# A squared-ReLU feed-forward block: x tile 0 loaded in two pieces, three tiles transposed ahead of chunk 0, shared tail transposes, a copy on ScalarE

## The chip, the cores and the metric

The kernel runs on one core of a Trainium2 chip. The metric is the device time of one execution in microseconds (us), smaller is better. Each kernel was executed several times; one execution of each was also recorded instruction by instruction (the profile, or trace). Loads are DMA transfers that an engine's queue issues: `nc.sync` is SyncE's queue (SPq in the traces), `nc.scalar` ScalarE's (ACTq). One execution below fell in a slow state, at a lower granted clock (0.853). Times in a trace count from the first instruction (the span); the device time is 1.8 to 2.0 us longer than the span.

## The reference

```python
B, S, D, F = 1, 2048, 576, 4608          # bf16: x, w1, b1, w2, b2
h = einsum("bsd,df->bsf", x, w1) + b1
r = where(h > 0, h, 0)
out = einsum("bsf,fd->bsd", r * r, w2) + b2
```

## The kernel before

Rows of x are worked on in four blocks of 512. The first product needs x transposed (D on the partitions). 576 is 4.5 times 128, so the last 64 rows of w1 ("tails") are handled by matmuls that use half of the array's rows, two at a time (64*128 in the timelines, where the others are 128*128; in the trace of before the first such pair, L203 and L205, starts at 9.849 and 9.853 us).

For the first block nothing is in SBUF (the on-chip memory that these loads fill) yet. An x tile is 128 rows of x. While the loads arrive, PE (the matrix engine) runs dummy matmuls (the warm-up), then transposes the four x tiles itself, and works off a first group of four 128-column output chunks, `k_outer`: for each 128 rows of D one `w1n` piece, in two halves of 256 x rows. Then come the rows of `a_rows(0)`: 16 steps `j`, each with 18 matmuls that take one 64-row half of the array each. Matmuls on the lower half (L188, later L196) read the piece of `w1_h` of half 0, those on the upper half (L190, later L198) the piece of half 1. Each step needs 288 KB of w1 and takes 1.94 us (nine pairs, 0.216 us apart in the trace of before).

```python
WARM = [512] * 6 + [128]                  # dummy matmuls on constants
...
load_x(nc.sync, 0)                        # 128 x 576 bf16, 144 KB
load_x(nc.scalar, 1)
load_w1n(nc.sync, 0)                      # 128 x 512 bf16, 128 KB
load_x(nc.scalar, 2)
load_w1n(nc.sync, 1)
load_x(nc.sync, 3)
for k in range(2, NK):
    load_w1n(nc.sync, k)
...
for (j0, j1) in [(0, 1), (1, 2), (2, 4), (4, 6), (6, 8), (8, 10), (10, 12)]:
    load_w1(nc.sync, 0, j0, j1)           # one half of the partitions each
    load_w1(nc.sync, 1, j0, j1)
    if j0 == 0:
        load_w1n8(nc.sync, 0)             # the tails of the first four chunks, 32 KB each
        load_w1n8(nc.sync, 1)
load_xT(1)                                # DMA transposes of the next x block
for (j0, j1) in [(12, 14), (14, 16)]:
    load_w1(nc.sync, 0, j0, j1)
    load_w1(nc.sync, 1, j0, j1)
...
# k_outer, in PE's order
for j in range(2):
    for k in range(NK): x_transpose(j, k)          # x tiles 0 and 1
for j in range(2):      x_transpose(j, NK)         # their tails
x_copies(0)
part(0, 0)                                         # four matmuls of 256 columns
for k in range(NK + 1): x_transpose(2, k)
part(0, 1); part(0, 2)
for k in range(NK + 1): x_transpose(3, k)
x_copies(1); dup_windows(0)                        # shifted copies, VectorE
part(0, 3); part(1, 0); make_b1T()
part(1, 1); part(1, 2); part(1, 3)
# then four tail matmuls, then a_rows(0)
```

## Time and profile before

| | before |
|---|---|
| device time | 290.71 us median of 3 (290.42 to 290.91) |
| the profiled execution | 291.46 us, span 289.6 |
| first transpose of PE | 3.77 us |
| first w1_h matmul | 10.29 us |

The first part of the page of the kernel before (engine, busy us and share, instructions) and the first line of its chain of waits:

```profile
PE 285.5 (99%) x2027; PEld 139.9 (48%) x2032; DVE 78.6 (27%) x176; ACT 96.7 (33%) x154; POOL 2.3 (1%) x10
...
PE 98%; DMA 1%; issue 0%; DVE 0%
```

PE is the whole kernel. The timeline of PE of the kernel before, in the head (start us, length us, engine, line, operation, output and inputs, shape, count; in brackets idle time of the engine before and what ended it):

```profile
0.78 2.83 PE L63 MATMUL wps<-const-bfloat16-1.0 128*128 128x512 bf16 x7 [0.78 <-PEq L344]
3.77 1.25 PE L149 MATMUL tb<-ident,x_sb 128*128 128x128 bf16 x10 [0.17 <-DMA x_sb<-in_x_dram]
4.87 1.01 PE L227 MATMUL pn<-xTw,w1n 128*128 128x256 bf16 x4
5.68 0.74 PE L149 MATMUL tb<-ident,x_sb 128*128 128x128 bf16 x5
6.21 1.19 PE L227 MATMUL pn<-xTw,w1n 128*128 128x256 bf16 x8
7.24 0.44 PE L149 MATMUL tb<-ident,x_sb 128*128 128x128 bf16 x5
7.51 1.04 PE L227 MATMUL pn<-xTw,w1n 128*128 128x256 bf16 x8
8.39 0.22 PE L166 MATMUL b1T_ps<-ident,b_rows 128*128 128x128 bf16 x1
8.44 1.47 PE L227 MATMUL pn<-xTw,w1n 128*128 128x256 bf16 x12
...
10.29 0.38 PE L188 MATMUL ph<-xTw,w_h 64*128 64x512 bf16 x1
```

Two things are to be read here. PE never waits long: after its first transpose no line has a wait in brackets. And the pace changes: five transposes take 0.74 us at 5.68 and 0.44 us at 7.24, four matmuls of 256 columns 1.01 us at 4.87, eight 1.04 us at 7.51. Single starts in the trace are 0.107 us apart for a transpose and 0.213 us for a 256-column matmul at first, and 0.056 and 0.109 later, about half of that: the document calls the first half clock and the second full clock. The trace's clock record begins at 6.51 us, with 1.00 ("the rise"); before that it holds nothing, so half clock is read from the steps. From 10.29 us to the last matmul (286.66 us) it takes 276.37 us.

Issues of loads on SyncE's queue (SPq) in the same trace; the `w_h` lines are the pieces of w1_h:

```profile
3.60 1.40 SPq L82 DMA_DIRECT2D w_h<-in_w_dram  x2
5.05 1.29 SPq L79 DMA_DIRECT2D w1n<-in_w_dram  x2
...
24.21 1.97 SPq L82 DMA_DIRECT2D w_h<-in_w_dram  x3
```

And, from the view of DMA issues of the kernel before in a window about 1.2 us, w1n piece 0 (size, us from issue to landing):

```profile
w1n<-in_w_dram SPq DMA_DIRECT2D x1, 128.0 KB, 3.1
```

It is issued at 1.20 and so lands at 4.3 us, before PE asks for it at 4.87. The queue's first w1_h piece is issued at 3.60 us, its last ones from 24.21 on.

### The profile page before, as it was taken

The page shows a single profiled execution, that of the slowest core. Times are in us where ns is not written, and L with a number is a line of the kernel's source. Part 1 is how long each engine was busy: PE and PEld are TensorE (multiplying, and loading weights), DVE is VectorE, ACT ScalarE, POOL GpSimd, SP SyncE. Part 2 cuts the span into 40 slices and gives each one's busy share as a digit, 9 for nine tenths or more (in the row PEclk, how much of TensorE's full clock was granted, in tenths as well). Part 3 has the DMA queues.
Part 4 walks back from the last instruction along what each step waited for, and adds up shares of the span by engine and source line. Part 5 has one row for each costly group of instructions (what it writes and reads, how often), then busy time and mean ns, then how long its engine had stood idle before and what let it go on. Part 6 is the DMA issues. An engine that isn't in the chain of part 4 may idle for free.

```text
span 289.6 us, 4693 instructions
## 1 busy us (share of the span) xinstructions
PE 285.5 (99%) x2027; PEld 139.9 (48%) x2032; DVE 78.6 (27%) x176; ACT 96.7 (33%) x154; POOL 2.3 (1%) x10
## 2 busy tenths in 40 slices
PE   8999999999999999999999999999999999999996
PEld 5544444444444555555544444444444455555555
DVE  1644554444500200000015444444440001100001
ACT  2566666666500000000027666666670000000000
POOL 3000000000000000000000000000000000000000
PEclk9999999999999999999999999999999999999999
DMA  7999999400001200000000000000000110000000
GB/s 198 221 245 188 308 389 212 92 0 2 0 14 25 52 16 18 16 16 18 16 16 2 1 2 0 2 0 2 0 2 0 36 38 16 16 16 19 33 16 18
DMA packets 31605, 16.52 MB, mean 57 GB/s; under 512 B 15700, under 2 KB 31584, under 8 KB 31584
## 3 DMA queue, kind: packets, MB, share of 16 engines
q1 hardware_dynamic: 31232, 15.91, 22.3%
q10 hardware_dynamic: 288, 0.30, 0.4%
q8 instruction: 16, 0.26, 0.4%
q14 instruction: 5, 0.04, 0.0%
q0 software_dynamic: 64, 0.01, 0.0%
HBM read 11.36 MB, written 2.36 MB: 47 GB/s over the span
## 4 chain that ended last, share of the span: by engine, by line
PE 98%; DMA 1%; issue 0%; DVE 0%
PE ph L188 42%; PE po L289 38%; PE pt L270 11%; PE pn L209 4%; PE pn L227 1%; DMA x_sb<-in_x_dram 1%; PE tb L149 1%; PE ph L190 1%; PE pn L203 1%; DVE o_sb L291 0%; PE b1T_ps L166 0%; PE pn L205 0%
## 5 line engine op out<-in xcount | busy, mean ns | idle before, releaser
L190 PE MATMUL ph<-xTw,w_h 64*128 64x512 bf16 x576 | 124.6, 376 | 0.0
L188 PE MATMUL ph<-xTw,w_h 64*128 64x512 bf16 x576 | 124.6, 376 | 0.0
L289 PE MATMUL po<-w_sb,hT 128*128 128x448 bf16 (+2 forms) x612 | 109.4, 341 | 0.0
L176 ACT ACTIVATE r<-ph,b1T 128x512 bf16<-128x512 f32 x128 | 81.1, 685 | 41.6 <-PE ph L190 41.6
L188 PEld LDWEIGHTS <-w_h 64*128 64x128 bf16 x576 | 54.1, 94 | 68.3
L289 PEld LDWEIGHTS <-hT 128*128 128x128 bf16 x612 | 58.5, 98 | 51.0
L177 DVE TENSOR_TENSOR hT<-r 128x512 bf16<-128x512 bf16 x144 | 61.2, 426 | 75.9 <-ACT r L176 75.5
L190 PEld LDWEIGHTS <-w_h 64*128 64x128 bf16 x576 | 54.1, 94 | 0.0
L291 DVE TENSOR_TENSOR o_sb<-po,b_bc 128x448 bf16<-128x448 f32 (+2 forms) x17 | 10.2, 597 | 125.8 <-PE po L289 125.8
L270 PE MATMUL pt<-hT,w_sb 128*128 128x512 bf16 x142 | 31.3, 379 | 0.1
L176 ACT ACTIVATE r<-pn,b1T 128x512 bf16<-128x512 f32 x16 | 10.3, 688 | 61.0 <-PE pn L205 59.6
L270 PEld LDWEIGHTS <-w_sb 128*128 128x128 bf16 x144 | 14.1, 98 | 17.0
L273 ACT ACTIVATE oT<-pt,b2T 128x512 bf16<-128x512 f32 x4 | 2.8, 688 | 28.3 <-PE pt L270 28.3
L209 PE MATMUL pn<-xTw,w1n 128*128 128x512 bf16 x45 | 10.4, 379 | 0.4 <-issue 0.3
L209 PEld LDWEIGHTS <-w1n 128*128 128x128 bf16 x48 | 4.5, 98 | 6.0 <-issue 0.8
L227 PE MATMUL pn<-xTw,w1n 128*128 128x256 bf16 x32 | 4.6, 295 | 0.0
L63 PE MATMUL wps<-const-bfloat16-1.0 128*128 128x512 bf16 (+1 forms) x7 | 2.8, 582 | 0.8 <-PEq L344 0.8
L227 PEld LDWEIGHTS <-w1n 128*128 128x128 bf16 x32 | 3.3, 107 | 0.5
L156 DVE COPY xTw<-tb 128x256 bf16<-128x256 bf16 x4 | 1.1, 292 | 6.7 <-PE tb L149 6.7
L119 DVE COPY xTw<-xTw 64x2048 bf16<-64x2048 bf16 x4 | 2.8, 690 | 0.2
L120 DVE COPY xTw<-xTw 64x2048 bf16<-64x2048 bf16 x4 | 2.7, 687 | 0.1
L149 PE MATMUL tb<-ident,x_sb 128*128 128x128 bf16 x20 | 2.4, 288 | 0.2 <-DMA x_sb<-in_x_dram 0.2
(23 smaller groups left out, 15.2 us busy)
## 6 DMA issues: line engine op xcount, KB each, us to landing
w_sb<-in_w_dram SPq DMA_DIRECT2D x4, 1296.0 KB, 12.7
w_h<-in_w_dram SPq DMA_DIRECT2D x14, 288.0 KB, 6.2
out_dram<-o_sb SPq DMA_DIRECT2D x15, 112.0 KB, 1.7
w_h<-in_w_dram SPq DMA_DIRECT2D x4, 144.0 KB, 3.5
w1n<-in_w_dram SPq DMA_DIRECT2D x4, 128.0 KB, 3.9
out_dram<-ot SPq DMA_DIRECT2D x4, 128.0 KB, 2.0
x_sb<-in_x_dram ACTq DMA_DIRECT2D x2, 144.0 KB, 2.9
x_sb<-in_x_dram SPq DMA_DIRECT2D x2, 144.0 KB, 3.4
```

The lines of the kernel that those rows point to most:

```text
L63: keep(nc.tensor.matmul(wps[:, 0:n], lhsT=ones[:, 0:P], rhs=ones[:, 0:n], start=True, stop=True))
L149: keep(nc.tensor.transpose(bank[:, slot, qc], xs[:, j, c0:c0 + P], ident[:]))
L176: keep(nc.scalar.activation(out=r[:], in_=bank[:], func=ACT.Relu, bias=b1T[:, ft:ft + 1], scale=1.0))
L177: keep(nc.vector.tensor_tensor(out=hTs[sb][:, ft, :], in0=r[:], in1=r[:], op=ALU.mult))
L188: keep(nc.tensor.matmul(bx[:], lhsT=w1_h[0:H, LO_C[i], jc], rhs=xT[0:H, LO_W[i], :], start=(i == 0), stop=(i == NC - 1)))
L190: keep(nc.tensor.matmul(by[:], lhsT=w1_h[H:P, UP_C[i], jc], rhs=xT[H:P, UP_W[i], :], start=(i == 0), stop=(i == NC - 1)))
L203: keep(nc.tensor.matmul(banks[2 * i][:], lhsT=w1n8[0:H, i, :], rhs=xT[0:H, SPC, :], start=start, stop=stop, skip_group_check=order == "k_o ...
L209: keep(nc.tensor.matmul(banks[g][:], lhsT=w1n[:, k, g * P:(g + 1) * P], rhs=xT[:, O + k, :], start=start, stop=stop))
L227: keep(nc.tensor.matmul(banks[g][:, hc], lhsT=w1n[:, k, g * P:(g + 1) * P], rhs=xT[:, O + k, hc], start=(h == 0 and k == 0), stop=False, s ...
L270: keep(nc.tensor.matmul(pt[:], lhsT=w2_sb[:, ft, DM:D], rhs=hT[:, ft, :], start=(i == 0), stop=(i == NFT - 1)))
L289: keep(nc.tensor.matmul(po[:, 0:d1 - d0], lhsT=hT[:, ft, jj * P:(jj + 1) * P], rhs=w2_sb[:, ft, d0:d1], start=(i == 0), stop=(i == NFT - 1)))
L291: keep(nc.vector.tensor_tensor(out=o_sb[:, d0:d1], in0=po[:, 0:d1 - d0], in1=b2_bc[:, d0:d1], op=ALU.add))
```

## The change

The intent is to start PE earlier and to take work and waits out of the head. x tile 0 comes in two column pieces on two queues; the warm-up is shorter to match; three x tiles are transposed before the first chunk, so that copies have time; the tail columns of two tiles share one transpose; a shifted copy moves to ScalarE. Loads are rearranged with it: more go through ScalarE's queue, `w1n8` is loaded in full for both halves (64 KB each) and ahead of `w1_h`, the last `w1_h` pieces and the w2 pieces are merged into larger ones, and b1 and b2 leave GpSimd's queue.

```diff
-    WARM = [512] * 6 + [128]
+    WARM = [512] * 5 + [256]
...
-    load_x(nc.sync, 0)
-    load_x(nc.scalar, 1)
-    load_w1n(nc.sync, 0)
+    load_x(nc.sync, 0, 0, 2 * P)
+    load_x(nc.scalar, 0, 2 * P, D)
+    load_x(nc.sync, 1)
     load_x(nc.scalar, 2)
-    load_w1n(nc.sync, 1)
-    load_x(nc.sync, 3)
-    for k in range(2, NK):
-        load_w1n(nc.sync, k)
+    load_w1n(nc.sync, 0, 1)
+    load_x(nc.scalar, 3)
+    load_w1n(nc.sync, 1, 2)
+    load_w1n(nc.scalar, 2, 3)
+    load_w1n(nc.sync, 3, 4)
...
+    keep(nc.scalar.dma_start(out=b1_rows[0:NFT, :], in_=b1.rearrange("(ft p) -> ft p", p=P)))
+    for h in range(2):
+        load_w1n8(nc.sync, h)               # now 64 KB each
...
+    def dup_windows_first():
+        keep(nc.scalar.copy(out=xT0[0:H, E:E + 3, :], in_=xT0[H:P, O:O + 3, :]))
+    def transpose_tails():
+        ... two transposes in place of four, four small copies, two shifted copies on VectorE
...
-                for j in range(2):
-                    for k in range(NK):
-                        x_transpose(j, k)
-                ...
+                for j in range(3):
+                    x_transpose(j)
                 part(0, 0)
-                for k in range(NK + 1):
-                    x_transpose(2, k)
+                x_transpose(3)
+                dup_windows_first()
                 part(0, 1)
                 part(0, 2)
-                ...
+                transpose_tails()
                 part(0, 3)
-                part(1, 0)
-                make_b1T()
-                for k in range(1, NK):
+                for k in range(NK):
                     part(1, k)
+                    if k == 1:
+                        make_b1T()
...
-        if j0 == 0:
-            load_w1n8(nc.sync, 0)
-            load_w1n8(nc.sync, 1)
     load_xT(1)
-    for (j0, j1) in [(12, 14), (14, 16)]:
+    for (j0, j1) in [(12, 16)]:
```

(Not shown here: the banks of PSUM, the layout of `w1n8`, the loads of b2 and w2.)

## The prediction

> **What bounds the kernel now.** The page's first part has PE busy 285.5 of 289.6 us (99%); the chain of work that ended last is 98% PE. From 10.29 us on (first L188 matmul in the timeline) 512-column matmuls start every 0.216 us until the last output. The change touches nothing there; w2 comes in three pieces instead of four, but is first used after 76 us. So only the head, 0 to 10.29 us, can change, plus new waits in the first rows.

> **The head before** (timeline, PE): warm-up matmuls 0.78 to 3.61; first transpose at 3.77, right after x tile 0 landed at 3.73 (3.0 us from issue). Then PE works nearly back to back until 10.29; its largest later gap is about 0.1 us, ahead of the L203 pair. Until about 6.5 us the steps are those of half clock (0.107 us per transpose, 0.213 per 256-column matmul), after it 0.056 and 0.109. [...] So the head is work-bound: 20+1 transposes, 32 half-width matmuls, 4 narrow ones.

> **What changes, costed.**
> - x tile 0 in two pieces on two queues: 144 KB instead of 288 KB ahead of the first transpose. From 2.9 to 3.7 us DMA moved about 350 GB/s, so an estimated 0.35 to 0.4 us less: first transpose at about 3.4. The shorter warm-up (ends about 3.1) fits. But this time is won at half clock: if the clock rises at 6.5 as before, 0.35 us earlier is worth about 0.18.
> - Two transposes fewer (19 against 21): 0.11 us.
> - Three tiles transposed ahead of chunk 0: no PE work removed, only waits, of which there is about 0.1 us. Tile 3 should land at about 5.0 instead of 6.1; it is wanted at about 5.6 to 6.1.
> - The shifted copy on ScalarE (64x1536) should take 1.4 to 1.9 us (estimate from its 0.376 us at 256 columns and 0.685 at 512) and end near 8.6 to 9.0; first read near 10.8. Off the chain. DVE's four tail copies (about 0.28 us each) end near 8.6, ahead of the pairs at about 9.5.
> - w1n8 is 128 KB instead of 64, ahead of w1_h, whose first pieces land up to 0.8 us later than 7.3 to 8, still before 9.9.
> - b1 is issued by ScalarE after its table load (about 4.0) and should land by 7 to 8; wanted at about 8.5.

> Sum on the critical path: 0.2 + 0.1 + 0.1, about 0.4 us; first w1_h matmul at about 9.9 instead of 10.29.

> **Prediction:** 290.3 us, 289.6 to 291.0 (8 in 10). Faster by over 2%: 0.005; within 2%: 0.985; slower by over 2%: 0.01. 2% would be 5.8 us, more than half of the head.

> **What would show it.** First transpose at 3.3 to 3.5 us; x tile 3 landed before 5.5; full-rate steps from about 6.5; no PE wait over 0.15 us after 4.5; first w1_h matmul at 9.7 to 10.1; from there to the end the same 279.3 us, to 0.2.

> **What would make it wrong.** The gap after the shorter warm-up, or waits for x tile 1, [...]. [...] the three timings before spread by 0.5 us, as much as the gain. PE waiting on b1 or w1n pieces. An early rise would make the gain larger, up to 0.8 us.

## The result, and the profile after

| | before | after |
|---|---|---|
| device time, median | 290.6 us (6 runs, 290.42 to 290.91) | 291.66 us (6 runs, 291.26 to 293.21) |
| ratio of the fast runs | | 1.0042, 95% interval 1.0020 to 1.0065 |
| the profiled execution | 291.46 us | 291.26 us |
| first transpose | 3.77 us | 3.07 us |
| first w1_h matmul | 10.29 us | 9.76 us |

Ratios here and below are the mean time of one kernel's fast runs over that of the other's fast runs of the same rounds, so they are not quite the ratio of the medians. The kernel became slower by 0.4%, clear of noise, and its times spread four times as far. The predicted 290.3 and the range to 291.0 were missed.

The page of the changed kernel, the same parts:

```profile
PE 285.5 (99%) x2029; PEld 139.4 (48%) x2029; DVE 79.3 (27%) x181; ACT 97.5 (34%) x153; POOL 1.5 (1%) x9
...
PE 97%; DMA 1%; SPq 0%; DVE 0%; issue 0%
```

The timeline of PE of the changed kernel in the head:

```profile
0.77 2.50 PE L63 MATMUL wps<-const-bfloat16-1.0 128*128 128x512 bf16 x6 [0.77 <-PEq L343]
3.07 1.64 PE L150 MATMUL tb<-ident,x_sb 128*128 128x128 bf16 x12
5.14 0.79 PE L232 MATMUL pn<-xTw,w1n 128*128 128x256 bf16 x4 [0.43 <-DMA w1n<-in_w_dram]
5.77 0.39 PE L150 MATMUL tb<-ident,x_sb 128*128 128x128 bf16 x4
5.99 1.04 PE L232 MATMUL pn<-xTw,w1n 128*128 128x256 bf16 x8
6.87 0.28 PE L163 MATMUL tl<-ident,xs 128*128 128x128 bf16 x2
6.98 1.47 PE L232 MATMUL pn<-xTw,w1n 128*128 128x256 bf16 x12
...
9.76 0.38 PE L196 MATMUL ph<-xTw,w_h 64*128 64x512 bf16 x1
```

PE starts 0.70 us earlier, but now it waits: 0.43 us without any work for w1n piece 0, and a little ahead of tile 1's transposes. In this execution the clock happened to rise at 5.55 us. The piece is issued at 1.66 us and lands at 5.1; from the view of DMA issues of the changed kernel about 1.65 us:

```profile
w1n<-in_w_dram SPq DMA_DIRECT2D x1, 128.0 KB, 3.4
```

The issues of SyncE's queue and what that queue waited for (waiter, what for: us in total, times, longest):

```profile
3.32 1.20 SPq L79 DMA_DIRECT2D w1n<-in_w_dram  x2
5.32 2.70 SPq L82 DMA_DIRECT2D w_h<-in_w_dram  x4
```

```profile
SPq L82 <- DMA x_sb<-in_x_dram: 0.8, 1, 0.8
```

The first piece of w1_h is issued at 5.32 us instead of 3.60 (and the merged last ones from 25.07, in the trace). Two w1n8 loads now stand ahead of it, and then the queue itself waits 0.8 us for an x tile to land. (In the same view of the kernel before, no load waits for a landing in this stretch.) The operands in the two traces show what this wait is. In the changed kernel that w1_h load waits for semaphore 106, which it then uses for its own completion; x tile 3's load, issued on ScalarE's queue at 1.66 us, has the same semaphore and landed at 5.30, and the w1_h load was issued at 5.32. (In after_look the same wait took 1.1 us.) In the kernel before the first w1_h load waits for semaphore 100, that of x tile 1, which had landed at 3.52 when the load was issued at 3.60. So between these two programs the landing that the first w1_h load has to wait for changed too. What comes of the later start is seen at step j = 12. PE's timeline of the kernel before there, where the two halves start together:

```profile
33.60 0.38 PE L188 MATMUL ph<-xTw,w_h 64*128 64x512 bf16 x1
33.60 0.38 PE L190 MATMUL ph<-xTw,w_h 64*128 64x512 bf16 x1
33.82 0.38 PE L188 MATMUL ph<-xTw,w_h 64*128 64x512 bf16 x1
```

and of the changed kernel:

```profile
33.06 0.38 PE L196 MATMUL ph<-xTw,w_h 64*128 64x512 bf16 x1
33.41 0.39 PE L198 MATMUL ph<-xTw,w_h 64*128 64x512 bf16 x1
33.41 0.39 PE L196 MATMUL ph<-xTw,w_h 64*128 64x512 bf16 x1
```

L198 should start with the L196 of 33.06. It starts 0.35 us later, when the merged piece of half 1 has landed (33.37 us in the trace). The lower half has run one step ahead by then and the two halves stay staggered until the next full-height matmul at 72.8 us, where the step is given back. From the first w1_h matmul to the last matmul it is 276.72 us instead of 276.37: the full 0.35 us.

So the fastest of the six executions shows 0.53 us won in the head and 0.35 us lost later. It doesn't show why the others took 291.5 to 293.2, nor why before's timed executions were faster than its profiled one. That was for the experiments.

### The profile page after: what moved, and what is told of

Read it like the earlier page. It is cut to its first block, busy times and chain, and to the rows that moved or that the text cites. A ratio compares the mean times of both kernels' runs of the same rounds, so it can differ in the third digit from the quotient of the medians.

```text
span 289.3 us, 4699 instructions
## 1 busy us (share of the span) xinstructions
PE 285.5 (99%) x2029; PEld 139.4 (48%) x2029; DVE 79.3 (27%) x181; ACT 97.5 (34%) x153; POOL 1.5 (1%) x9
## 4 chain that ended last, share of the span: by engine, by line
PE 97%; DMA 1%; SPq 0%; DVE 0%; issue 0%
PE po L287 38%; PE ph L196 29%; PE ph L198 14%; PE pt L268 11%; PE pn L217 4%; PE pn L232 1%; DMA w1n<-in_w_dram 1%; PE pn L211 1%; SPq L72 0%; PE pn L213 0%; DVE o_sb L289 0%; PE tb L150 0%; PE tl L163 0%; PE b1T_ps L174 0%
## 5 line engine op out<-in xcount | busy, mean ns | idle before, releaser
L198 PE MATMUL ph<-xTw,w_h 64*128 64x512 bf16 x576 | 124.8, 376 | 0.0
L196 PE MATMUL ph<-xTw,w_h 64*128 64x512 bf16 x576 | 124.8, 376 | 0.0
L196 PEld LDWEIGHTS <-w_h 64*128 64x128 bf16 x576 | 54.1, 94 | 46.9
L198 PEld LDWEIGHTS <-w_h 64*128 64x128 bf16 x576 | 54.0, 94 | 21.6 <-DMA w_h<-in_w_dram 0.5
L289 DVE TENSOR_TENSOR o_sb<-po,b_bc 128x448 bf16<-128x448 f32 (+2 forms) x17 | 10.2, 597 | 125.8 <-PE po L287 125.8
L213 PE MATMUL pn<-xTw,w1n 64*128 64x512 bf16 x8 | 2.4, 378 | 0.0
L211 PE MATMUL pn<-xTw,w1n 64*128 64x512 bf16 x8 | 2.4, 378 | 0.0
```

The costliest lines, as they stand in the source:

```text
L196: keep(nc.tensor.matmul(bx[:], lhsT=w1_h[0:H, LO_C[i], jc], rhs=xT[0:H, LO_W[i], :], start=(i == 0), stop=(i == NC - 1)))
L198: keep(nc.tensor.matmul(by[:], lhsT=w1_h[H:P, UP_C[i], jc], rhs=xT[H:P, UP_W[i], :], start=(i == 0), stop=(i == NC - 1)))
L211: keep(nc.tensor.matmul(banks[2 * i][:], lhsT=w1n8[0:H, 2 * i * P:(2 * i + 1) * P], rhs=xT[0:H, SPC, :], start=start, stop=stop, skip_grou ...
L289: keep(nc.vector.tensor_tensor(out=o_sb[:, d0:d1], in0=po[:, 0:d1 - d0], in1=b2_bc[:, d0:d1], op=ALU.add))
```

## The experiments

Four things are quoted from each trace: when the clock rose, the start of the first w1_h matmul, the time from it to the last matmul (276.37 us where nothing stalls), and the time of that execution. Medians are of 5 or 6 executions, each beside executions of the kernel before on the same chip (median 290.8 to 290.9 there).

| run | median us | ratio to before | profiled execution us | rise us | first w1_h us | to last matmul us |
|---|---|---|---|---|---|---|
| before | 290.6 | | 291.46 | 6.51 | 10.29 | 276.37 |
| after | 291.66 | 1.0042 | 291.26 | 5.55 | 9.76 | 276.72 |
| before_again | 290.89 | 1.0000 | (slow) | | | |
| after_again | 291.72 | 1.0024 | 292.98 | 8.87 | 11.81 | 276.37 |
| after_look | one run | | 293.25 | 9.15 | 11.77 | 276.67 |
| split_w1 | 293.37 | 1.0078 | 293.05 | 9.36 | 11.72 | 276.37 |
| before_merged | 291.38 | 1.0013 | 290.91 | 5.14 | 9.55 | 276.53 |
| fill_gaps | 292.32 | 1.0044 | 292.82 | 4.26 | 9.67 | 278.36 |
| before_newloads | 291.15 | 1.0010 | 290.99 | 3.92 | 9.67 | 276.37 |
| oldloads | 291.61 | 1.0023 | 291.80 | 5.96 | 9.89 | 277.12 |
| old_warmup | 292.05 | 1.0043 | 292.00 | no record; about 5.8 by the steps | 9.90 | 277.25 |
| w1_first | 291.52 | 1.0044 | 293.92 | see below | 12.59 | 276.37 |
| mended | 290.89 | 1.0006 | 291.33 | 6.77 | 10.20 | 276.37 |
| mended_fill | 291.96 | 1.0035 | 290.90 | 4.44 | 9.56 | 276.37 |
| mended_fill_look | one run | | 291.55 | 5.84 | 10.22 | 276.37 |
| before_w1late | 291.85 | 1.0028 | 292.04 | 6.79 | 10.41 | 276.80 |
| before_shortwarm | 291.97 | 1.0031 | 292.17 | 8.31 | 11.10 | 276.37 |
| early_w1n0 | 291.66 | 1.0023 | 291.66 | 4.31 | 10.46 | 276.37 |

### before_again and after_again: controls

No edit.

> Control: the kernel before, unchanged, timed against itself. Theory A (a real loss in the changed kernel: the merged last w1 pieces land too late) and theory B (the half-clock stretch of the changed kernel lasts longer in most executions): ratio 1.000, interval inside 0.999 to 1.001, median 290.4 to 290.8. Theory C (the changed kernel's times carry an offset of the measurement, because its six were taken another way than those of before): ratio about 1.003, median about 291.4.

> The changed kernel, unchanged, for its spread and a second trace. A: the trace again shows a gap of PE at the w1_h matmuls of j = 12 (about 33 us), of 0.1 to 2 us, differing from execution to execution; median 291.3 to 292, spread over 0.5 us. B: no or the same small gap at 33 us, but the half-clock stretch ends at another time than 5.5 us and the time goes with it. C: as before_again to 0.2 us.

before_again: ratio 1.0000 (0.9986 to 1.0014). One of its executions, the profiled one, slow (335.78 us, granted clock 0.853), is left out. The median, 290.89, lies a little above the expected 290.4 to 290.8, but so do the executions of before beside it (290.92). Theory C falls. after_again: the loss repeats (291.72, 1.0024, interval 1.0010 to 1.0039). Its trace, an execution of 292.98 us, has no gap at 33 us, but a rise at 8.87 us: B's picture. A's gap was not there. The changed kernel has at least two kinds of execution.

### split_w1: the last w1_h pieces in two again

```diff
-    for (j0, j1) in [(12, 16)]:
+    for (j0, j1) in [(12, 14), (14, 16)]:
```

> The changed kernel with the last w1 piece of each half loaded in two again (j 12 to 14, then 14 to 16), nothing else. A: no PE gap near 33 us, the pieces for j = 12 land before about 31.5, median 290.0 to 290.6, 0.8 to 1.5 us below after_again, spread below 0.4 us. B or C: the same as after_again to 0.2 us (in the profile at most the 0.35 us that the gap cost there comes back).

293.37 us, all five executions between 292.67 and 293.52: slower, not faster, and in the range of no theory. The traced one rose at 9.36 us and had no gap; as its first w1_h matmul came only at 11.72 us, that says little for the edit. A alone falls. Why all five came in the late kind, and only about three of twelve of the changed kernel, stays open; the edit touches nothing before 24 us.

### before_merged: the merged piece alone, in the kernel before

```diff
-    for (j0, j1) in [(12, 14), (14, 16)]:
+    for (j0, j1) in [(12, 16)]:
```

> The kernel before with the last w1 pieces merged as in the changed kernel, nothing else. The merged upper piece is issued at about 24.9 and should land at 31.5 to 33 us, wanted at 33.6. A: a stall in some executions only, median 290.6 to 291.4, spread larger than before_again's. B or C: the same as before_again to 0.2 us.

291.38 us, ratio 1.0013 (1.0000 to 1.0026): in A's range, near the edge of what can be told. Its trace was an early one (rise 5.14, first w1_h matmul 9.55), and there the stretch to the last matmul is 0.16 us longer than 276.37: a short stall at j = 12. This trace tells something else too: the same head as before, with the rise 1.37 us and the first transpose 0.25 us earlier, ends 0.74 us earlier, and the execution took 290.91 us. So before's profiled execution, with its rise at 6.51, was a late one of its kind.

### fill_gaps: PE kept busy where it waited

```diff
-                for j in range(3):
-                    x_transpose(j)
+                x_transpose(0)
+                fill(5)          # matmuls of 128 columns on constants, overwritten later
+                x_transpose(1)
+                x_transpose(2)
+                fill(8)
                 part(0, 0)
```

> The changed kernel with filler matmuls on constants (128 columns, results overwritten) in the two places where PE waited: five after the transposes of tile 0, eight ahead of chunk 0. No load is moved. B, now put so: the half-clock stretch ends at the end of the first 3.41 us window in which PE idles less than about 0.5 us (0.43 rose, 0.63 and 0.72 did not); the waits for x tile 1 and for w1n piece 0 cost the changed kernel that window in most executions. B expects the rise before 7 us in the trace, first w1_h matmul at 9.0 to 10.2, median 290.3 to 291.1 (0.7 to 1.5 below after_again), although PE has 13 matmuls more to do. If the waits cost only their own length, the fillers sit in their shadow and the median stays at 291.5 to 292.0.

The 3.41 us of B is the length of two stretches in the clock record of w1_first (below). Its idle times were read from traces: 0.43 us in after (PE busy 2.98 of the 3.41 us before its rise, 2.14 to 5.55), 0.63 in split_w1, 0.72 in after_again.

The rise came at 4.26 us and the first w1_h matmul at 9.67, as B wanted, and still the median was 292.32. The timeline of PE of fill_gaps says where the time went, at step j = 2:

```profile
13.55 0.38 PE L196 MATMUL ph<-xTw,w_h 64*128 64x512 bf16 x1
15.54 0.39 PE L198 MATMUL ph<-xTw,w_h 64*128 64x512 bf16 x1 [1.61 <-DMA w_h<-in_w_dram]
```

PE, early in the rows, ran into the w1_h supply and waited (the next step comes 1.99 us after the last); the piece landed at 15.49. So mending the clock alone brings the other loss out.

### before_newloads, oldloads, old_warmup: which part of the change

before_newloads puts the changed loads of x and w1n (order, queues, pieces) into the kernel before. oldloads puts those of before, and its warm-up, into the changed kernel. old_warmup puts only the warm-up length of before (`[512] * 6 + [128]`) into the changed kernel.

> The kernel before with only the changed order, queues and pieces of the x and w1n loads. B: PE idles 0.4 to 1.2 us ahead of chunk 0, waiting for w1n piece 0 (landing 5.1 to 6.0 instead of 4.0 to 4.3), the rise comes after 8 us in part of the executions, median 291.3 to 292.5, spread over 0.8. If the loss came from the changed order of PE's or the other engines' work: 290.5 to 291.0, as before.

> The changed kernel with the order and queues of the x and w1n loads, and the warm-up length, of before; everything else of the change stays. B: no PE wait over 0.3 us ahead of chunk 0, rise before 7 us, first w1_h matmul at 9.0 to 10.0, median 290.2 to 290.9. If the loss lies in the rest of the change: 291.4 or more.

> The changed kernel with the longer warm-up of before (6x512+128 columns instead of 5x512+256), nothing else. B: the wait for x tile 1 is filled (PE busy to about 4.0), the one for w1n piece 0 stays at 0.1 to 0.9 us, so fewer executions lose the window: median 290.6 to 291.5, below after_again's. If the shorter warm-up has no part in it: 291.5 to 292.0.

All three medians missed what B expected of them; that of oldloads fits the other expectation, "in the rest of the change", those of before_newloads and old_warmup neither. before_newloads: 291.15, ratio 1.0010 (0.9998 to 1.0022), nearly no loss, although w1n piece 0 was late (4.82 us) and PE waited for it; it rose early (3.92) and its w1_h supply was before's. oldloads: 291.61 (1.0023, 1.0011 to 1.0035), the loss stays without the new x loads. old_warmup: 292.05, all five between 292.00 and 292.58. In the traces of oldloads and old_warmup the clock rose early enough to have the first w1_h matmul at 9.9, and they lost 0.75 and 0.88 us at j = 12. The wait in oldloads, in the view of waits between 20 and 40 us:

```profile
PEld L197 <- DMA w_h<-in_w_dram: 0.9, 1, 0.9
PE ph L197 <- DMA w_h<-in_w_dram: 0.4, 1, 0.4
```

B as the only cause falls with this. The theory after these eight: two losses that hide each other. An execution with an early rise meets the late supply; one with a late rise doesn't.

### w1_first, mended, mended_fill, before_w1late: the supply

w1_first gives the changed kernel the w1_h order of before:

```diff
-    for h in range(2):
-        load_w1n8(nc.sync, h)
...
         load_w1(nc.sync, 1, j0, j1)
+        if j0 == 0:
+            load_w1n8(nc.sync, 0)
+            load_w1n8(nc.sync, 1)
     load_xT(1)
-    for (j0, j1) in [(12, 16)]:
+    for (j0, j1) in [(12, 14), (14, 16)]:
```

mended is that edit on oldloads, mended_fill that edit on fill_gaps. before_w1late is the reverse edit (w1n8 of 64 KB ahead of w1_h, last pieces merged) on the kernel before.

> The changed kernel with the w1_h supply alone as before: the two w1n8 loads go behind the first pair of w1_h pieces again (still in their new 64 KB size), and the last pieces are split again. Theory now (A+B): the changed kernel loses in two ways that exclude each other in part. When the clock rises in time, PE reaches the w1_h rows early and runs into a w1 supply that starts 1.5 us later (first piece issued at 5.1 to 5.5 instead of 3.6), stalling 0.3 to 2 us at j = 2 or j = 12; when PE's waits in the head delay the rise to about 9 us, it loses 1.5 to 2 us there and no stall shows. Here: first w1_h piece issued before 4.7 us, no PE gap over 0.1 us in the w1_h rows, median 290.3 to 291.4; a late rise can still show (then 292.5 or more). If only the clock matters: 291.6 or more, as after_again.

> The changed kernel with both mended: w1_h supply as in w1_first, x and w1n loads and warm-up length as in oldloads. What stays of the change: the transposes (two fewer), shared tails, copies on ScalarE, banks, b1 and b2 on other queues. A+B: no gaps in the w1_h rows, rise before 7 us, median 290.0 to 290.7, below before or equal. If the loss lies in what stays: above 291.2.

> The changed kernel with its own early x loads, the fillers of fill_gaps and the w1_h supply of w1_first. A+B: first transpose at 3.07, rise before 7 us, no gaps in the w1_h rows, median 290.0 to 290.8, 1.5 to 2.3 below fill_gaps. If the stall of 1.99 us seen in fill_gaps has another cause than the late supply, it stays and the median is 291.5 to 292.5.

> The kernel before with the changed w1 supply: w1n8 at 64 KB a half and ahead of w1_h, last pieces merged; x and w1n loads and all of PE's order stay. A+B: first w1_h piece issued at 4.6 to 5.2 us instead of 3.6, PE gaps of 0.2 to 1.5 us at j = 2 or j = 12, median 291.3 to 292.2. If the supply is no cause: 290.8 to 291.1.

No stall in the w1_h rows is left in any trace of w1_first, mended or mended_fill: 276.37 us in all, against 277.12 and 278.36 of oldloads and fill_gaps. mended takes 290.89 (1.0006, 0.9994 to 1.0018), 0.72 below oldloads, from which it differs by the supply alone (by their ratios to before, 0.0017 of 291 us, it is 0.5); it was hoped to end below before and only equals it. before_w1late shows the supply as a cause in the other kernel: 291.85 (1.0028, 1.0015 to 1.0040), first w1_h piece issued at 4.84 us, 0.43 us lost at j = 12 in its trace. The supply is a cause. Two things stay open here: the mean loss, 0.0028 of 291 us, is 0.8 us, and no trace tells where the rest of it lies; and how much is the late start and how much the merge is not separated (the merge alone, in before_merged, gave 1.0013, and the intervals overlap).

The medians of the two versions that keep the new x loads missed what was expected: w1_first's 291.52 lies between its two ranges, and mended_fill's 291.96 is far from 290.0 to 290.8, which only its traced execution (290.90) came near. So the supply is not all of the loss.

w1_first's single executions go up to 293.92. That slowest one was traced. In the view of chosen stretches (us, busy us of the engines with counts, granted clock "PEclk", DMA share, GB/s):

```profile
0.80:3.60 2.80, 2.80 (x10) 1.15 (x10) 0.11 (x1) 0.97 (x1) 0.43 (x2) 1.00 0.64 161
3.70:7.00 3.30, 1.30 (x14) 0.91 (x14) 0.88 (x4) 0.41 (x2) 0.52 (x2) 1.00 0.98 272
7.10:10.40 3.30, 3.30 (x21) 2.43 (x18) 1.44 (x6) 2.12 (x3) 0.00 (x0) 0.50 0.46 109
10.50:12.00 1.50, 1.50 (x16) 1.30 (x14) 1.27 (x4) 0.00 (x0) 0.00 (x0) 1.00 0.80 212
```

The clock rose at 3.65 us, PE was then busy for only 1.30 of 3.30 us (w1n piece 0 landed at 6.45), and the clock fell back to 0.50 for the whole next stretch, 7.07 to 10.48 us, though PE was busy through all of it. In the clock record both stretches, 3.65 to 7.07 and 7.07 to 10.48, are 3.41 us long. (In the first line the view prints 1.00, but there is no clock record before the rise; the steps of the warm-up, 0.43 us for 512 columns, are those of half clock.)

### before_shortwarm: idle time alone

```diff
-    WARM = [512] * 6 + [128]
+    WARM = [512] * 4
```

> The kernel before with only the warm-up cut to 4x512 columns. It ends near 2.5 us and PE then idles about 1.0 to 1.2 us until x tile 0 lands at 3.5 to 3.7; no load, no other work is moved, and PE waited for that tile before as well. If idle time of PE in a clock window costs the kernel the full clock for one window more (B): the rise comes at 6.6 to 10 us in most executions, median 291.8 to 292.8. If waits cost only their own length: 290.6 to 291.1, as before.

This is the clean test of the clock part: in the kernel before, with no load and no other work changed. Timeline of PE of before_shortwarm:

```profile
0.78 1.86 PE L63 MATMUL wps<-const-bfloat16-1.0 128*128 128x512 bf16 x4 [0.78 <-PEq L344]
3.64 1.25 PE L149 MATMUL tb<-ident,x_sb 128*128 128x128 bf16 x10 [1.00 <-DMA x_sb<-in_x_dram]
4.74 1.01 PE L227 MATMUL pn<-xTw,w1n 128*128 128x256 bf16 x4
...
11.10 0.38 PE L188 MATMUL ph<-xTw,w_h 64*128 64x512 bf16 x1
```

The first transpose is no later than before (3.64 against 3.77), yet the rise is at 8.31 and the first w1_h matmul at 11.10. The median is 291.97 (1.0031, 1.0010 to 1.0051), the six executions 291.33 to 292.73. One us of idle time that delayed nothing cost 1.1 us by the medians, 0.9 by the ratio. Rival "waits cost only their own length" falls.

### early_w1n0 and two more looks

early_w1n0 is mended_fill with w1n piece 0 second on SyncE's queue, x tile 1 second on ScalarE's, tiles 2 and 3 and the other w1n pieces on SyncE's, chunk 0 ahead of tile 2's transposes, and seven fillers instead of thirteen.

> An attempt at a better version: x tile 0 in two pieces is kept; w1n piece 0 comes second on SP's queue and x tile 1 second on ScalarE's; the w1_h supply is as before; chunk 0 goes ahead of tile 2's transposes again; four fillers after tile 0, three after tile 1. A+B: w1n piece 0 lands at 3.9 to 4.4, no PE gap over 0.2 us in the head, rise before 7 us, no gap in the w1_h rows, median 290.1 to 290.8. If the late w1n piece 0 is no cause of mended_fill's 291.96: 291.6 or more.

> A second look at mended_fill, whose trace showed an undisturbed head at 290.9 while its five other executions took 291.7 to 292.5. If the late and uneven landing of w1n piece 0 is behind that: w1n piece 0 lands after 5.8 us here, PE waits more than 0.4 us for it in spite of the fillers, time 291.6 to 292.5. If it is the w1_h supply: gaps at j = 1 to 3 of the w1_h rows.

> A third trace of the changed kernel. A+B: either a rise of the clock after 8 us and no gap in the w1_h rows, or a rise before 7 us and a gap of 0.1 to 2 us in them, near j = 2 or j = 12; time 291.2 to 293.3.

early_w1n0 failed: 291.66, where it was expected if the late w1n piece 0 were no cause of mended_fill's 291.96. The run doesn't decide that: w1n piece 0 landed at 4.09 as hoped and the clock rose at 4.31, but PE then waited for what had been put behind: its trace has 1.06 us of idle time after the rise, most of it ahead of tile 3, which landed at 6.42. mended_fill_look fits neither of its two expectations: w1n piece 0 landed at 5.22, there was no gap in the head or in the rows, and it took 291.55. The fillers themselves can explain this trace: PE was still at half clock (rise 5.84), so thirteen fillers took 1.39 us, and they ended at 5.74, half a microsecond after the piece had landed. In the first trace of mended_fill the rise was at 4.44, and the head ended 0.65 us earlier. Fillers are not free.

after_look, timeline of PE:

```profile
3.08 0.63 PE L150 MATMUL tb<-ident,x_sb 128*128 128x128 bf16 x4
3.91 1.03 PE L150 MATMUL tb<-ident,x_sb 128*128 128x128 bf16 x8 [0.21 <-DMA x_sb<-in_x_dram]
5.66 1.04 PE L232 MATMUL pn<-xTw,w1n 128*128 128x256 bf16 x4 [0.71 <-DMA w1n<-in_w_dram]
6.48 0.63 PE L150 MATMUL tb<-ident,x_sb 128*128 128x128 bf16 x4
```

Both waits, a rise at 9.15 us, first w1_h matmul at 11.77; and in addition a stall of 0.30 us at 35 us, because the merged piece landed only at 35.33. The two losses exclude each other less than theory A+B said.

## Why the prediction was wrong

**An account of the head.** In the four traces below the end of the head is, to about 0.1 us, the sum of four terms: the first transpose, the idle time of PE after it, the work at full clock, and half of the time that PE worked at half clock. The work is 21 transposes, 32 matmuls of 256 columns and two paired tail steps: 21 x 0.056 + 32 x 0.109 + 2 x 0.216 = 5.10 us before, and 4.98 after with its 19 transposes.

| trace | first transpose | idle | work | half of half-clock work | sum | measured |
|---|---|---|---|---|---|---|
| before (rise 6.51) | 3.77 | 0.16 | 5.10 | 1.34 | 10.37 | 10.29 |
| after (rise 5.55) | 3.07 | 0.91 | 4.98 | 0.84 | 9.80 | 9.76 |
| after_look (rise 9.15) | 3.08 | 1.43 | 4.98 | 2.37 | 11.86 | 11.77 |
| before_shortwarm (rise 8.31) | 3.64 | 0.16 | 5.10 | 2.31 | 11.21 | 11.10 |

(Idle is the sum of the steps beyond their nominal length, so it is more than the bracketed waits, which count from the end of the last matmul.) The change won 0.70 us in the first term and 0.12 in the third, and gave 0.75 to 1.6 back in the second (1.75 us of idle time in after_again). The fourth is the clock.

Point by point:

What the runs showed in place of the prediction: the early start was lost again to w1n piece 0 within two microseconds; then either a later rise of the clock or the w1_h supply, at times both, took 0.3 to 2 us more. Mending the supply and the x loads together (mended) brings the time back to before's, and no version tried beats before.

**What stays open.** Of the twelve executions of the changed kernel, nine took 291.26 to 292.02 us and only the fastest of these was traced, so how the two losses share the middle ones is not known. Why all of split_w1's executions are of the late kind is open. So is why w1n piece 0 landed anywhere between 4.8 and 6.5 us in kernels with the same order of loads. The device time exceeds the span by 1.92 to 1.93 us in all traces of the changed kernel and by 1.77 to 1.86 in those of before and its variants; this 0.1 us was not looked into.

## What to carry to other kernels

When a load is moved forward, follow the ones that it pushes back, each to the moment of its use, and not only the first of a stream: a stream that was just ahead of its reader must be checked at its later pieces and at any merged one, against a reader that arrives earlier. In the first ten microseconds of this kernel idle time of the matrix engine cost more than it delayed: in before_shortwarm 1.0 us that delayed nothing cost 0.9 us, and its trace has the rise at 8.31 us, where before's has it at 6.51. Look there for work that fills such waits and doesn't end after the data has come (in mended_fill_look the fillers ended half a microsecond after it). And look whether the profiled execution is a typical one before costing anything from it.
